# Sequence transform in one tile shape, alternating between the column halves

## The chip, the cores and the metric

One core of a Trainium2 chip. The metric is the time on the device, in microseconds, of one execution. Engines are called as the profile calls them: PE (TensorE matmul), PEld (its weight loads), DVE (VectorE), ACT (ScalarE), POOL (GpSimd), SP (the queue that issues transfers).

## The reference

Four batches, 1088 positions, 128 features (4 heads of 32). Three stages follow each other:

```python
# attention with a feature map, per head: phi(x) = (S1 x) outer (S2 x), 64 values
num = q_p @ (k_p.T @ v);  den = q_p @ sum(k_p);  x = num / (den + 1e-6)
# Fourier mixing and a channel block
X = np.fft.fft(np.fft.fft(x, axis=1), axis=2)      # over positions, then features
u = x + np.real(X)
x = u + relu(norm(u) @ w_ch1) @ w_ch2
# gated block with a spatial product over the 1088 positions
h = relu(x @ w_in);  a, v = h[..., :512], h[..., 512:]
out = (a * (w_spatial @ norm(v) + b_spatial)) @ w_out
```

All is float32. The scale factors of S1, S2 come as float64.

## The kernel before

The kernel first converts its weights from float64 bit patterns (`from_f64`, `weight`, on ACT, DVE and POOL), then runs for every batch `keys` and `queries` (the attention), `fourier_seq` and `fourier_feat` (the real part of the two-dimensional Fourier transform), `channel` and `spatial`. The attention and Fourier parts of batches 1 to 3 run early, and PE's gaps there are filled with products of the spatial part of batch 0 (tile `ac`, lines 569 to 571); the engines' instruction order is fixed when the program is built. Later batches interleave `channel(b + 1)` with `spatial(b)`, which runs to the end.

The Fourier part uses symmetry. Tokens s, S - s, 544 - s and 544 + s are kept together ("four groups"), so that sums and differences fold the position axis to a quarter, in an even and an odd parity, and the feature axis to 64 cosine and 63 sine columns and one extra column (feature 64). `fourier_seq` works like this (lines 404 to 453):

- line 408: a product folds the 9th row block (`rp`), ACT copies it to `rs_` (line 412);
- lines 417 to 434: DVE and POOL make the sums and differences: `eo`, `fe`, then `l_` (cosine part `l_[:, 0]`, sine part `l_[:, 1]`, by parity and row block), `lz` (the extra column, 32 wide), `lr` and `lzr` (leftover positions: 64 rows, of which each product takes 32). Line 415 and 416 zero a column of `l_` and of `lr` for each batch, on POOL;
- lines 438 to 453: for each parity nine products into `dps` (name `dft`), in 274 columns: for each of two row blocks a cosine product (128 rows, 64 columns, left half of the array), a sine product (right half) and the extra column (128 rows, 32 columns, at column 96); then the same three for the leftover positions, with 32 rows. ACT copies the result to every second column of `tb` (line 453).

`fourier_feat` (lines 455 to 475) multiplies `tb` by the feature table `dd` and adds the result to `ub`. In the profile each float32 matmul is two instructions, each with its weight load. `xtile` gives PSUM tiles: tag `acc` (two buffers) for batch 0, tag `x` (three) for the others. `warm` issues products of zeros that keep the clock up.

Positions are stored in the order of `_token_rows`; the host arranges inputs, tables (`_layout`) and the output by it.

Of the kernel before, what the change touches and what calls it, by code (L numbers as in the profile page):

```python
# [7 lines left out]
F32 = mybir.dt.float32  # L8
# [8 lines left out]
DM = 128  # L17
FF = 512
P = 128
NT = 9  # L20
CH = [(0, 384, 3), (384, 384, 3), (768, 320, 2)]
NCOL = 274
TW = 564
REM = [257 + i for i in range(15)] + [272, None, 0] + [None] * 14


def _groups(s):
    return [s % S, (S - s) % S, (544 - s) % S, (544 + s) % S]


def _token_rows():
    rows = []
    for blk in range(2):
        for g in range(4):
            rows += [_groups(1 + 128 * blk + i)[g] for i in range(128)]
    for g in range(4):
        rows += [_groups(257 if s is None else s)[g] for s in REM]
    return rows


def _rem_unique():
    return (
        [0 * 32 + i for i in list(range(16)) + [17]]
        + [1 * 32 + i for i in range(16)]
        + [2 * 32 + i for i in list(range(15)) + [17]]
        + [3 * 32 + i for i in range(15)]
    )

# [7 lines left out]
def fourier_attention_gmlp_kernel(  # L56
# [18 lines left out]
    nc = tc.nc  # L75
    V, A, T, G = nc.vector, nc.scalar, nc.tensor, nc.gpsimd
    mm = T.matmul
# [22 lines left out]
    ub, x2, marks = {}, {}, {}  # L100
# [4 lines left out]

    # spatial weights of one block of output positions, split into two float32r parts
    def spatial_load(pool, c, stage):
# [30 lines left out]

    # ------------------------------------------------------------------ channel part of one sequence
    def rstd(pool, mv, n, tag, nb=1):  # L140
# [134 lines left out]

    # ------------------------------------------------------------------ attention and Fourier mixing
    sa = ExitStack()
# [5 lines left out]
    trr = ca.tile([P, NCOL], F32, name="trr")  # L283
    dd = ca.tile([P, 2, DM], F32, name="dd")
    kvz = [ca.tile([P, 2, 66], F32, name=f"kvz{i}") for i in range(2)]
    lz = ca.tile([P, 2, 2, 32], F32, name="lz")
    lzr = ca.tile([64, 32], F32, name="lzr")
    tb = {}
# [6 lines left out]
    def from_f64(raw, n, out, fast):  # L295
        # mantissa rounded to float32 in [1, 2], times a power of two with the sign
        w = raw.rearrange("p (n two) -> p n two", two=2)
# [106 lines left out]
    def fourier_seq(b):  # L404
        # fold over the sequence, then over the features, then over the sequence halves
        xb = ub[b][:, 0:8, :].rearrange("p (k e f) d -> p (k e) f d", k=2, e=2)
        rp = xtile(b, [P, DM], "rp")
        mm(out=rp, lhsT=rfold, rhs=ub[b][:, 8, :], start=True, stop=True)
        if b == 0:
            warm(10)  # L410
        rs_ = ca.tile([P, DM], F32, tag="rs", name="rs_")
        A.copy(out=rs_, in_=rp)
        lr = ca.tile([P, 65], F32, tag="lr", name="lr")
        l_ = ca.tile([P, 2, 2, 2, 65], F32, tag="l_", name="l_")
        G.memset(l_[:, 1, :, :, 64:65], 0.0)
        G.memset(lr[64:128, 64:65], 0.0)
        for i, op in enumerate((ALU.add, ALU.subtract)):
            eo = ca.tile([P, 4, DM], F32, tag="eo", bufs=2, name="eo")
            V.tensor_tensor(out=eo, in0=xb[:, :, 0, :], in1=xb[:, :, 1, :], op=op)
            fe = ca.tile([P, 4, 64], F32, tag="fe", bufs=2, name="fe")  # L420
            if i == 0:
                G.tensor_copy(out=fe[:, :, 0:1], in_=eo[:, :, 0:1])
            V.tensor_tensor(out=fe[:, :, 1:64], in0=eo[:, :, 1:64], in1=eo[:, :, 127:64:-1], op=op)
            rows = slice(64 * i, 64 * i + 64)
            V.tensor_tensor(out=lr[rows, 1:64], in0=rs_[rows, 1:64], in1=rs_[rows, 127:64:-1], op=op)
            ev = fe.rearrange("p (k e) d -> p k e d", e=2)
            eov = eo.rearrange("p (k e) d -> p k e d", e=2)
            for par in range(2):
                o2 = ALU.add if par == i else ALU.subtract
                V.tensor_tensor(out=l_[:, i, par, :, i:64], in0=ev[:, :, 0, i:64], in1=ev[:, :, 1, i:64], op=o2)  # L430
                if i == 0:
                    G.tensor_tensor(out=lz[:, :, par, 31:32], in0=eov[:, :, 0, 64:65], in1=eov[:, :, 1, 64:65], op=o2)
        G.tensor_copy(out=lr[0:64, 0:1], in_=rs_[0:64, 0:1])
        G.tensor_copy(out=lzr[:, 31:32], in_=rs_[0:64, 64:65])
        t_ = tb[b] = ca.tile([P, TW], F32, tag="tb", bufs=2, name="tb")
        G.memset(t_[:, 548:TW], 0.0)
        tbv = t_[:, 0:550].rearrange("p (n two) -> p n two", two=2)
        for par in range(2):
            dps = xtile(b, [P, 512], "dft")
            for kt in range(3):  # L440
                for g in (0, 1, 2) if kt < 2 else (0, 2, 1):
                    cs = g % 2
                    q = slice(64 * cs + 32 * par, 64 * cs + 32 * par + 32)
                    if g < 2:
                        lh = l_[:, cs, par, kt, cs:64 + cs] if kt < 2 else lr[q, cs:64 + cs]
                    else:
                        lh = lz[:, kt, par, :] if kt < 2 else lzr[q, :]
                    rh = tr[:, kt, 2 * cs + par, :] if kt < 2 else trr[q, :]
                    o0, w = ((0, 64), (64, 64), (96, 32))[g]
                    mm(out=dps[o0:o0 + w, 0:NCOL], lhsT=lh, rhs=rh, start=(kt == 0 and g < 2),  # L450
                       stop=(kt == 2 and g < 2), tile_position=(0 if kt < 2 else q.start, o0))
            dst = tbv[:, 1:275, 0] if par == 0 else tbv[:, 0:274, 1]
            A.copy(out=dst, in_=dps[:, 0:NCOL])

    def fourier_feat(b):
        t_ = tb.pop(b)
        for blk in range(2):
            u_ = xtile(b, [P, 4, DM], "ups")
            for e in range(2):
                p0 = (275 if e else 1) + 128 * blk  # L460
                mm(
                    out=u_[:, 2 * e:2 * e + 2, :].rearrange("p g d -> p (g d)"),
                    lhsT=t_[:, p0:p0 + 128],
                    rhs=dd.rearrange("p g d -> p (g d)"),
                    start=True,
                    stop=True,
                )
            ux = ub[b][:, 4 * blk:4 * blk + 4, :]
            V.tensor_tensor(out=ux, in0=u_, in1=ux, op=ALU.add)
        u_ = xtile(b, [P, DM], "urm")  # L470
        for g in range(4):
            p0 = 257 if g < 2 else 531
            mm(out=u_[32 * g:32 * g + 32, :], lhsT=t_[:, p0:p0 + 32], rhs=dd[:, g % 2, :], start=True, stop=True,
               tile_position=(0, 32 * g))
        V.tensor_tensor(out=ub[b][:, 8, :], in0=u_, in1=ub[b][:, 8, :], op=ALU.add)
# [4 lines left out]
    A.activation(out=rt, in_=cst[:, 0:1], func=ACTF.Sqrt)  # L480
    # zero products that keep the tensor engine's clock up while it waits
    wz = a1
# [10 lines left out]
    from_f64(raw0, 64, sb_s, True)  # L493
    for z in (*kvz, lz, lzr):
        G.memset(z, 0.0)
# [52 lines left out]

    # ------------------------------------------------------------------ spatial part
    def spatial(b):  # L550
# [70 lines left out]
def _layout(q, k, v, S1, S2, moe_w_ch1, moe_w_ch2, moe2_w_in, moe2_w_spatial, moe2_b_spatial, moe2_w_out):  # L621
# [24 lines left out]
    a["wout"] = moe2_w_out.reshape(4, P, DM).transpose(1, 0, 2).reshape(P, FF)  # L646
    tpos = np.full(549, -1)
    for pos in range(1, 273):
        tpos[pos] = pos
    tpos[274] = 0  # L650
    for pos in range(275, 547):
        tpos[pos] = 818 - pos
    tpos[548] = 544
    lists = [tpos[2:549:2], tpos[1:549:2]]

# [11 lines left out]
    both = lambda ss: np.concatenate([table(ss, np.cos), table(ss, np.sin)], 1)  # L667
    full = both(list(range(1, 257))).reshape(2, P, 4, NCOL).transpose(1, 0, 2, 3)
    a["trig"] = full.astype(f32)
    a["trig_r"] = both(REM).transpose(1, 0, 2).reshape(P, NCOL).astype(f32)  # L670
    e = np.arange(P)
    dc = np.zeros((P, 2, P))
    for d in range(64):
        dc[d, :, :] = np.cos(2 * np.pi * ((d * e) % P) / P)
    for d in range(1, 64):
        sn = np.sin(2 * np.pi * ((d * e) % P) / P)
        dc[63 + d, 0, :] = -sn
        dc[63 + d, 1, :] = sn
    dc[127, :, :] = 1.0 - 2.0 * (e % 2)
    a["ddft"] = dc.astype(f32)  # L680
# [7 lines left out]
    for o in range(4):  # L688
        for g in range(4):
            for i in range(32):  # L690
                pm[32 * g + i, 2, 32 * o + i] = sgn[o, g]
    a["perm"] = pm
# [26 lines left out]
```

## Time and profile before

| | us |
|---|---|
| median of 3 runs | 484.94 |
| lowest and highest run | 482.51, 486.26 |
| span of the profiled execution (first to last instruction) | 481.6 |

The profiled execution's own time is given by its span alone; the runs are timed from outside. The profile is one execution, taken on the chip, with 7520 instructions. Busy times are sums over an engine's instructions, and matmuls overlap in the pipeline, so a busy PE is not PE at its peak. The chain of waits goes back from the last instruction to whatever released it. Times in the timeline count from the start of the span.

### The profile page before, as it was taken

To read this page: it belongs to the slowest core of one execution; us is meant where nothing else is said; L and a number is where in the kernel's file an instruction comes from. 1 tells how busy PE (TensorE), PEld (TensorE's weight loads), DVE (VectorE), ACT (ScalarE), POOL (GpSimd) and SP (SyncE) were. 2 spreads that over 40 slices of the span, in tenths; PEclk is the share of its full clock that TensorE was granted. 3 is DMA by queue.
4 is the path that set the end of the run, shared out by engine and by line. 5 is a ranking of instruction groups with operands and counts; after the bars stand their busy time and mean duration, and the time that the engine had idled before them with its cause. 6 is when DMAs were issued, how large, how long until landed. Compare 5 with 4: busy or idle time off the path is not lost.

```text
span 481.6 us, 7520 instructions
## 1 busy us (share of the span) xinstructions
PE 462.5 (96%) x2909; PEld 410.7 (85%) x2909; DVE 269.9 (56%) x677; ACT 193.0 (40%) x448; POOL 67.0 (14%) x105
## 2 busy tenths in 40 slices
PE   7889789999999997999999999999999999999996
PEld 6846678848948947989999999999999999999995
DVE  3576898849534518578963635496363547421221
ACT  3525687436322206445643333364243335311121
POOL 2044495426011104000000000000000000000000
PEclk9789899999999999899999999999999999999999
DMA  7950134004100004000000000000000000000000
GB/s 238 349 199 17 49 92 125 18 1 122 46 1 1 1 1 140 0 1 0 19 14 1 0 18 1 0 18 14 1 1 18 0 2 18 14 1 16 1 16 15
DMA packets 13007, 19.16 MB, mean 40 GB/s; under 512 B 1446, under 2 KB 11564, under 8 KB 12844
## 3 DMA queue, kind: packets, MB, share of 16 engines
q1 hardware_dynamic: 12972, 18.69, 12.2%
q8 instruction: 23, 0.38, 0.3%
q14 instruction: 12, 0.10, 0.1%
HBM read 16.45 MB, written 2.23 MB: 39 GB/s over the span
## 4 chain that ended last, share of the span: by engine, by line
PE 86%; DVE 5%; DMA 3%; ACT 2%; issue 1%; POOL 1%; SPq 1%; POOLq 0%; DVEq 0%; ACTq 0%
PE ac L569 13%; PE ac L571 13%; PE ac L570 13%; PE dft L450 8%; PE nm L387 3%; PE abp L331 2%; PE v_ps L244 2%; PE v_ps L246 2%; PE qps L376 2%; PE v_ps L245 2%; PE u_ps L564 2%; PE u_ps L562 2%; PE c L217 2%; PE ac L577 2%; PE ac L576 2%; PE u_ps L563 2%
## 5 line engine op out<-in xcount | busy, mean ns | idle before, releaser
L569 PE MATMUL ac<-wsh,vh 128*128 128x384 f32 (+1 forms) x384 | 126.9, 330 | 0.0
L571 PE MATMUL ac<-wsh,vlo 128*128 128x384 f32 (+1 forms) x384 | 126.6, 330 | 0.0
L570 PE MATMUL ac<-wsl,vh 128*128 128x384 f32 (+1 forms) x384 | 126.5, 330 | 0.0
L569 PEld LDWEIGHTS ac<-wsh,vh 128*128 128x128 f32 x384 | 72.2, 188 | 1.4 <-issue 0.8
L570 PEld LDWEIGHTS ac<-wsl,vh 128*128 128x128 f32 x384 | 72.2, 188 | 1.2 <-issue 0.4
L571 PEld LDWEIGHTS ac<-wsh,vlo 128*128 128x128 f32 x384 | 72.3, 188 | 1.2 <-issue 1.0
L580 DVE TENSOR_TENSOR uh<-ac,uh 128x384 f32<-128x384 f32 (+1 forms) x48 | 25.4, 530 | 55.5 <-PE ac L577 55.5
L566 ACT ACTIVATE uh<-u_ps 128x384 f32<-128x384 f32 (+1 forms) x48 | 22.6, 471 | 48.9 <-PE u_ps L564 46.9
L337 DVE TENSOR_TENSOR pp<-ab 128x768 f32<-128x768 f32 x23 | 26.1, 1150 | 17.5 <-ACT ab L333 16.5
L104 DVE TENSOR_TENSOR gl<-uh,gh 128x384 fp32r<-128x384 f32 (+1 forms) x48 | 25.6, 533 | 14.8 <-ACT gh L581 14.6
L235 POOL CAST xh<-xh 128x64 fp32r<-128x64 f32 x4 | 2.2, 543 | 202.2 <-ACT xh L232 202.2
L581 ACT CAST gh<-uh 128x384 fp32r<-128x384 f32 (+1 forms) x48 | 23.6, 492 | 10.8 <-DVE uh L580 10.5
L251 DVE BATCH_NORM_STATS2 bst<-vn 128x6 f32<-128x512 f32 x27 | 18.6, 693 | 16.7 <-ACT vn L249 16.6
L249 ACT ACTIVATE vn<-v_ps 128x512 f32<-128x512 f32 x27 | 16.0, 598 | 19.1 <-PE v_ps L246 18.6
L231 DVE TENSOR_TENSOR xt<-c,xt 128x384 f32<-128x384 f32 (+1 forms) x12 | 6.4, 530 | 27.4 <-PE c L217 27.4
L217 PE MATMUL c<-hl,w 128*128 128x384 f32 (+1 forms) x48 | 16.5, 345 | 1.1 <-DVE hl L210 1.1
L387 PE MATMUL nm<-kvz,qp 128*128 128x66 f32 x144 | 16.8, 274 | 0.0
L387 PEld LDWEIGHTS nm<-kvz,qp 128*128 128x128 f32 x144 | 16.7, 193 | 0.0
L272 ACT CAST vh<-vn 128x1024 fp32r<-128x1024 f32 x12 | 12.6, 1047 | 10.3 <-PE ac L570 8.3
L215 PE MATMUL c<-hh,w 128*128 128x384 f32 (+1 forms) x48 | 16.3, 340 | 0.0
L232 ACT CAST xh<-xt 128x384 fp32r<-128x384 f32 (+1 forms) x12 | 6.0, 497 | 25.7 <-DVE xt L231 25.7
L564 PE MATMUL u_ps<-sxl,wi 128*128 128x384 f32 (+1 forms) x48 | 15.9, 331 | 0.4 <-DVE sxl L104 0.4
(717 smaller groups left out, 961.1 us busy)
## 6 DMA issues: line engine op xcount, KB each, us to landing
wst<-in_wsp SPq DMA_DIRECT2D x18, 192.0 KB, 2.5
vx<-in_vt SPq DMA_DIRECT2D x12, 198.0 KB, 3.1
kt<-in_kT SPq DMA_DIRECT2D x12, 192.0 KB, 3.8
qt<-in_qT SPq DMA_DIRECT2D x12, 192.0 KB, 4.7
w2st<-in_wsp SPq DMA_DIRECT2D x9, 160.0 KB, 3.3
tr<-in_trig SPq DMA_DIRECT2D x1, 1096.0 KB, 8.4
wraw<-in_win SPq DMA_DIRECT2D x4, 256.0 KB, 6.3
wraw<-in_w SPq DMA_DIRECT2D x4, 256.0 KB, 4.9
```

The source lines that it names most:

```text
L104: eng.tensor_tensor(out=lo, in0=x, in1=hi.bitcast(F32), op=ALU.subtract)
L217: mm(out=c2[:, 0:n], lhsT=wpart("w2", 0, 128 * m, 128), rhs=hl[:, 0:n], start=False, stop=(m == 3))
L337: (G if [b, tag[0], c] in [[3, 'k', 2]] else V).tensor_tensor(out=pp, in0=a_.unsqueeze(3).to_broadcast([P, 12, 8, 8]), in1=b_.unsqueeze(2) ...
L387: mm(out=nm[:, t, 2 * pr:2 * pr + 2, :].rearrange("p h d -> p (h d)"), lhsT=qp[:, pr, 128 * t:128 * t + 128], rhs=z[:, pr, :], start=True, ...
L450: mm(out=dps[o0:o0 + w, 0:NCOL], lhsT=lh, rhs=rh, start=(kt == 0 and g < 2), stop=(kt == 2 and g < 2), tile_position=(0 if kt < 2 else q.s ...
L564: mm(out=h_[:, 0:n], lhsT=wpart("wi", 0, 128 * m, 128), rhs=xl[:, 0:n], start=False, stop=True)
L566: A.activation(out=uh[:, 0:n], in_=h_[:, 0:n], func=ACTF.Relu)
L569: mm(out=ac[:, 0:n], lhsT=vh[:, k, ms], rhs=wsh[c][:, k, :], start=(k == 0), stop=False)
L570: mm(out=ac[:, 0:n], lhsT=vh[:, k, ms], rhs=wsl[c][:, k, :], start=False, stop=False)
L571: mm(out=ac[:, 0:n], lhsT=vl[:, k, ms], rhs=wsh[c][:, k, :], start=False, stop=False)
L580: V.tensor_tensor(out=uh[:, 0:n], in0=ac[:, 0:n], in1=uh[:, 0:n], op=ALU.mult)
L581: A.copy(out=gh[:, 0:n], in_=uh[:, 0:n])
```

## The change

The position order is changed: the first 256 folded positions are split by parity (`MAIN`), the leftover ones are nine of each parity (`REST`), and the trigonometric tables, `perm` and `dd` are laid out anew on the host. Each parity then has a transform of its own with 274 columns stored one after the other in `tb[:, par, :]`.

The leftover operands are padded to 128 rows: `lrb` (zero outside the 32 rows of its part and parity) takes the place of `lr`, and `trr` is used whole. The extra column is moved into a 64 wide operand, in its last column (`lz`, 64 wide instead of 32; `lzr` goes). With the sine columns beginning at index 1 this makes every product 128 rows by 64 columns: three cosine products and five sine products for each parity, 16 in all instead of 18. They are issued in eight couples, one on the left half and one on the right half of the columns, in program order. Parity 1 has its sine part on the left and its cosine part on the right, so `dd` has a table for each parity. The copy of parity 0 stands after the fifth couple. The diff, cut to its core:

```diff
-    dd = ca.tile([P, 2, DM], F32, name="dd")
+    dd = ca.tile([P, 2, 2, DM], F32, name="dd")
-    lz = ca.tile([P, 2, 2, 32], F32, name="lz")
-    lzr = ca.tile([64, 32], F32, name="lzr")
+    lz = ca.tile([P, 2, 2, 64], F32, name="lz")
+    lrb = ca.tile([P, 2, 2, 64], F32, name="lrb")
...
-        lr = ca.tile([P, 65], F32, tag="lr", name="lr")
         l_ = ca.tile([P, 2, 2, 2, 65], F32, tag="l_", name="l_")
         G.memset(l_[:, 1, :, :, 64:65], 0.0)
-        G.memset(lr[64:128, 64:65], 0.0)
...
-            rows = slice(64 * i, 64 * i + 64)
-            V.tensor_tensor(out=lr[rows, 1:64], in0=rs_[rows, 1:64], in1=rs_[rows, 127:64:-1], op=op)
...
             for par in range(2):
...
+                rows = slice(64 * i + 32 * par, 64 * i + 32 * par + 32)
+                V.tensor_tensor(out=lrb[rows, i, par, 1 - i:64 - i], in0=rs_[rows, 1:64], in1=rs_[rows, 127:64:-1], op=op)
+                if i == 0:
+                    G.tensor_copy(out=lrb[rows, 0, par, 0:1], in_=rs_[rows, 0:1])
+                    G.tensor_copy(out=lrb[rows, 1, par, 63:64], in_=rs_[rows, 64:65])
-        G.tensor_copy(out=lr[0:64, 0:1], in_=rs_[0:64, 0:1])
-        G.tensor_copy(out=lzr[:, 31:32], in_=rs_[0:64, 64:65])
-        t_ = tb[b] = ca.tile([P, TW], F32, tag="tb", bufs=2, name="tb")
-        G.memset(t_[:, 548:TW], 0.0)
...
+        dps = [xtile(b, [P, 512], "dft") for _ in range(2)]
+        done = {}
+        def dft(par, sine, lhsT, rhs, last):
+            c0 = 64 * (sine ^ par)
+            m_ = mm(out=dps[par][c0:c0 + 64, 0:NCOL], lhsT=lhsT, rhs=rhs, start=(par, sine) not in done, stop=last,
+                    tile_position=(0, c0))
+            if done:
+                tc.keep_in_program_order(m_)
+            done[par, sine] = True
+        def cosines(par):
+            return [(par, 0, l_[:, 0, par, kt, 0:64], tr[:, kt, par, :], False) for kt in range(2)] + [
+                (par, 0, lrb[:, 0, par, :], trr, True)]
+        def sines(par):
+            return [(par, 1, l_[:, 1, par, kt, 1:65], tr[:, kt, 2 + par, :], False) for kt in range(2)] + [
+                (par, 1, lrb[:, 1, par, :], trr, False)] + [
+                (par, 1, lz[:, kt, par, :], tr[:, kt, par, :], kt == 1) for kt in range(2)]
+        tb[b] = ca.tile([P, 2, NCOL], F32, tag="tb", bufs=2, name="tb")
+        left, right = cosines(0) + sines(1), sines(0) + cosines(1)
+        for i, (x, y) in enumerate(zip(left, right)):
+            dft(*x)
+            dft(*y)
+            if i == 4:
+                A.copy(out=tb[b][:, 0, :], in_=dps[0][:, 0:NCOL])
+        A.copy(out=tb[b][:, 1, :], in_=dps[1][:, 0:NCOL])
...
-                    lhsT=t_[:, p0:p0 + 128],
-                    rhs=dd.rearrange("p g d -> p (g d)"),
+                    lhsT=t_[:, par, 146 * e:146 * e + 128],
+                    rhs=dd[:, par, :, :].rearrange("p g d -> p (g d)"),
...
-    nc = bacc.Bacc("TRN2", target_bir_lowering=False, num_devices=1)
+    nc = bacc.Bacc("TRN2", target_bir_lowering=False, num_devices=1, dynamic_dma_scratch_size=4096)
```

`lrb` is zeroed once at the start, as `lz` was.

## Rows read from the trace of the kernel before

**Rows 1.** The page, parts 1 and 4: busy engines, and the chain's shares.

```profile
PE 462.5 (96%) x2909; PEld 410.7 (85%) x2909; DVE 269.9 (56%) x677; ACT 193.0 (40%) x448; POOL 67.0 (14%) x105
PE 86%; DVE 5%; DMA 3%; ACT 2%; issue 1%; POOL 1%; SPq 1%; POOLq 0%; DVEq 0%; ACTq 0%
```

**Rows 2.** The chain of waits, start and length, first and last transform.

```profile
30.70 9.09 PE dft L450 x36
...
168.37 9.23 PE dft L450 x36
```

**Rows 3.** Windows, line 450 alone: length, PE, PEld, clock, DMA; last and sum.

```profile
168.30:177.60 9.30, 9.30 (x36) 2.80 (x36) 1.00 0.00 1
sum 39.10, PE 37.32 PEld 11.18; mean PE 9.33 PEld 2.79
```

**Rows 4.** Timeline of PE in batch 2: start, length, instructions, rows*columns, count.

```profile
136.56 0.68 PE L450 MATMUL dft<-tr,l__1452 128*64 128x274 f32 x4
137.18 0.65 PE L450 MATMUL dft<-tr,lz 128*32 128x274 f32 x2
137.75 0.67 PE L450 MATMUL dft<-trr,lr 32*64 32x274 f32 x2
138.35 0.64 PE L450 MATMUL dft<-trr,lzr 32*32 32x274 f32 x2
...
146.18 0.43 PE L473 MATMUL urm<-dd,tb 128*32 128x128 f32 x8
```

**Rows 5.** The same timeline in windows of 0.01 us, for single starts.

```profile
134.30 0.42 PE L450 MATMUL dft<-tr,l__1452 128*64 128x274 f32 x1
134.56 0.39 PE L450 MATMUL dft<-tr,l__1452 128*64 128x274 f32 x1
134.79 0.40 PE L450 MATMUL dft<-tr,l__1452 128*64 128x274 f32 x1
135.02 0.39 PE L450 MATMUL dft<-tr,l__1452 128*64 128x274 f32 x1
135.41 0.42 PE L450 MATMUL dft<-tr,l__1452 128*64 128x274 f32 x1
...
136.56 0.45 PE L450 MATMUL dft<-tr,l__1452 128*64 128x274 f32 x2
136.84 0.40 PE L450 MATMUL dft<-tr,l__1452 128*64 128x274 f32 x2
```

**Rows 6.** Timelines of batches 0 and 1: waits of POOL, DVE and ACT, in brackets.

```profile
39.90 0.09 POOL L416 MEMSET lr<- 64x1 f32 x1 [2.30 <-PE dft L450]
41.52 0.29 DVE L306 TENSOR_SCALAR ds<-wraw 128x256 int32<-128x256 int32 x1 [4.21 <-POOL dr L310]
...
106.93 0.41 ACT L453 COPY tb<-dft 128x274 f32<-128x274 f32 x1 [4.47 <-PE dft L450]
107.76 0.56 DVE L104 TENSOR_TENSOR wsl<-wst,wsh 128x384 fp32r<-128x384 f32 x1 [5.73 <-ACT wsh L124]
```

**Rows 7.** Weight loads, batch 2: timeline, and line 450's ns (least/median/most).

```profile
134.27 0.65 PEld L450 LDWEIGHTS dft<-tr,l__1452 128*64 128x64 f32 x4 [0.25 <-PE u_ps L563]
L450 PEld LDWEIGHTS dft<-tr,l__1452 x16: 132/136/138, 134.3 to 140.8; 128*64 128x64 f32 x16
```

**Rows 8.** Timelines: DVE ahead of the transform of batch 2; SP's issue of dd.

```profile
134.72 0.22 DVE L425 TENSOR_TENSOR lr<-rs__1449 64x63 f32<-64x63 f32 x1
134.97 0.49 DVE L430 TENSOR_TENSOR l__1452<-fe 128x126 f32<-128x126 f32 x2
15.21 0.35 SPq L513 DMA_DIRECT2D dd<-in_ddft  x1
```

**Rows 9.** Windows, all work: length, PE, PEld, DVE, ACT, POOL, clock, DMA, GB/s.

```profile
107.00:118.00 11.00, 10.52 (x107) 8.77 (x107) 10.00 (x12) 7.30 (x18) 8.57 (x9) 1.00 0.41 113
190.00:195.00 5.00, 2.56 (x14) 2.56 (x15) 3.13 (x9) 2.25 (x5) 1.22 (x2) 0.89 0.00 0
```

More of the change, by code (lines that the diff above doesn't have):

```diff
@@ L22, with _rest_tokens @@
 NCOL = 274
-TW = 564
-REM = [257 + i for i in range(15)] + [272, None, 0] + [None] * 14
+MAIN = [[2 + 2 * i for i in range(128)], [1 + 2 * i for i in range(128)]]
+REST = [[258 + 2 * i for i in range(7)] + [272, 0], [257 + 2 * i for i in range(8)] + [None]]
 def _groups(s):
     return [s % S, (S - s) % S, (544 - s) % S, (544 + s) % S]
+def _rest_tokens(par, v):
+    own = [_groups(257 if s is None else s) for s in REST[par]]
+    return [g[v] for g in own] + [g[2 + v] for g in own] + [257] * 14
 def _token_rows():
     rows = []
-    for blk in range(2):
+    for par in range(2):
         for g in range(4):
-            rows += [_groups(1 + 128 * blk + i)[g] for i in range(128)]
-    for g in range(4):
-        rows += [_groups(257 if s is None else s)[g] for s in REM]
+            rows += [_groups(s)[g] for s in MAIN[par]]
+    for par in range(2):
+        for v in range(2):
+            rows += _rest_tokens(par, v)
     return rows
 def _rem_unique():
[L42 to L47, printed above, removed]
+    seen, rows = set(), []
+    for par in range(2):
+        for v in range(2):
+            for i, t in enumerate(_rest_tokens(par, v)[:18]):
+                if REST[par][i % 9] is not None and t not in seen:
+                    seen.add(t)
+                    rows.append(64 * par + 32 * v + i)
+    return rows
 def _order():
@@ L431, in fourier_seq @@
                 if i == 0:
-                    G.tensor_tensor(out=lz[:, :, par, 31:32], in0=eov[:, :, 0, 64:65], in1=eov[:, :, 1, 64:65], op=o2)
-        G.tensor_copy(out=lr[0:64, 0:1], in_=rs_[0:64, 0:1])
-        G.tensor_copy(out=lzr[:, 31:32], in_=rs_[0:64, 64:65])
-        t_ = tb[b] = ca.tile([P, TW], F32, tag="tb", bufs=2, name="tb")
-        G.memset(t_[:, 548:TW], 0.0)
[L437 to L453, printed above, removed]
@@ new lines, in fourier_seq @@
+                    G.tensor_tensor(out=lz[:, :, par, 63:64], in0=eov[:, :, 0, 64:65], in1=eov[:, :, 1, 64:65], op=o2)
+                rows = slice(64 * i + 32 * par, 64 * i + 32 * par + 32)
[3 more added lines that the diff above has]
+                    G.tensor_copy(out=lrb[rows, 1, par, 63:64], in_=rs_[rows, 64:65])
@@ L455, in fourier_feat @@
+        A.copy(out=tb[b][:, 1, :], in_=dps[1][:, 0:NCOL])
     def fourier_feat(b):
         t_ = tb.pop(b)
-        for blk in range(2):
+        for par in range(2):
             u_ = xtile(b, [P, 4, DM], "ups")
             for e in range(2):
-                p0 = (275 if e else 1) + 128 * blk
                 mm(
                     out=u_[:, 2 * e:2 * e + 2, :].rearrange("p g d -> p (g d)"),
-                    lhsT=t_[:, p0:p0 + 128],
-                    rhs=dd.rearrange("p g d -> p (g d)"),
+                    lhsT=t_[:, par, 146 * e:146 * e + 128],
+                    rhs=dd[:, par, :, :].rearrange("p g d -> p (g d)"),
@@ L467, in fourier_feat @@
                 )
-            ux = ub[b][:, 4 * blk:4 * blk + 4, :]
+            ux = ub[b][:, 4 * par:4 * par + 4, :]
             V.tensor_tensor(out=ux, in0=u_, in1=ux, op=ALU.add)
         u_ = xtile(b, [P, DM], "urm")
[L471 to L474, printed above, removed]
+        for par in range(2):
+            for v in range(2):
+                o0 = 64 * par + 32 * v
+                mm(out=u_[o0:o0 + 32, :], lhsT=t_[:, par, 128:160], rhs=dd[:, par, v, :], start=True, stop=True,
+                   tile_position=(0, o0))
         V.tensor_tensor(out=ub[b][:, 8, :], in0=u_, in1=ub[b][:, 8, :], op=ALU.add)
@@ L493, in fourier_attention_gmlp_kernel @@
     from_f64(raw0, 64, sb_s, True)
-    for z in (*kvz, lz, lzr):
+    for z in (*kvz, lz, lrb):
         G.memset(z, 0.0)
@@ L646, in _layout @@
     a["wout"] = moe2_w_out.reshape(4, P, DM).transpose(1, 0, 2).reshape(P, FF)
[L647 to L654, printed above, removed]
+    lists = []
+    for par in range(2):
+        t = MAIN[par] + REST[par] + [None if s is None else 544 - s for s in REST[par]] + [544 - s for s in MAIN[par]]
+        lists.append(np.array([-1 if x is None else x for x in t]))
     def table(ss, fn):
@@ L667, in _layout @@
     both = lambda ss: np.concatenate([table(ss, np.cos), table(ss, np.sin)], 1)
-    full = both(list(range(1, 257))).reshape(2, P, 4, NCOL).transpose(1, 0, 2, 3)
+    full = both(MAIN[0] + MAIN[1]).reshape(2, P, 4, NCOL).transpose(1, 0, 2, 3)
     a["trig"] = full.astype(f32)
-    a["trig_r"] = both(REM).transpose(1, 0, 2).reshape(P, NCOL).astype(f32)
+    a["trig_r"] = both(REST[0] + REST[1] + [None] * 14).transpose(1, 0, 2).reshape(P, NCOL).astype(f32)
     e = np.arange(P)
[L672 to L679, printed above, removed]
+    cos = np.stack([np.cos(2 * np.pi * ((d * e) % P) / P) for d in range(64)])
+    sin = np.stack([np.sin(2 * np.pi * ((d * e) % P) / P) for d in range(1, 64)])
+    last = 1.0 - 2.0 * (e[None] % 2)
+    dc = np.zeros((P, 2, 2, P))
+    for v in range(2):
+        parts = [cos, (2 * v - 1) * sin, last]
+        dc[:, 0, v, :] = np.concatenate(parts)
+        dc[:, 1, v, :] = np.concatenate(parts[1:] + parts[:1])
     a["ddft"] = dc.astype(f32)
@@ L688, in _layout @@
     for o in range(4):
-        for g in range(4):
-            for i in range(32):
-                pm[32 * g + i, 2, 32 * o + i] = sgn[o, g]
+        for par in range(2):
+            for j in range(9):
+                for g in range(4):
+                    pm[64 * par + 32 * (g % 2) + 9 * (g // 2) + j, 2, 32 * o + 9 * par + j] = sgn[o, g]
     a["perm"] = pm
```

## The prediction

> **What bounds the kernel now.** I read the page first. PE is busy 462.5 of 481.6 us and carries 86% of the chain that ended last; no other engine is busy for more than 56% of the span [rows 1]. So time counts when it leaves PE, provided that PE doesn't then wait for a neighbour. The busy share alone doesn't prove this, because matmuls overlap and a matmul that takes twice too long looks just as busy. Next I followed the chain of waits in order of time: the sequence transform (line 450) stands on it in all four batches, almost without a break, from 30.70 to 39.79 us the first time and from 168.37 to 177.60 us the last [rows 2]. The windows over these four stretches give its price: 37.32 us of PE, 9.33 us a batch, at a granted clock of 1.00, the higher level of 2.4 GHz [rows 3]. The clock has nothing to give back there.
>
> Then I looked inside one transform, that of batch 2, in the timeline of PE [rows 4]. Each float32 matmul shows as two instructions, so 18 matmuls are 36. Two patterns are to be seen. A lone matmul between others of another shape (lz in 32 columns, lr over 32 rows, lzr over 32 rows by 32 columns) takes the engine 0.57 to 0.60 us before the next group can start: 137.18 to 137.75, 137.75 to 138.35. But where two matmuls of 128 rows by 64 columns follow each other, the cosine and the sine product of one row block, on different column halves, four instructions take 136.56 to 137.18, 0.62 us: no more than one. The starts show why [rows 5]: two instructions start together at 136.56 and the other two by 136.84. Where consecutive instructions work on the same half, they start 0.23 us apart (134.56, 134.79, 135.02). So 0.23 us is the work of one instruction, 0.46 that of one matmul, about 0.14 the price of a change of shape, and the two halves run side by side.
>
> The check on the sum: 36 instructions at 0.23 are 8.28; the two overlapping groups take off 2 x 0.46; some fourteen changes of shape at 0.14 add 1.96; that makes 9.32 against 9.33 measured. The transform's excess is thus changes of shape and halves that idle, not arithmetic.
>
> Last I looked at who stands behind it [rows 6]. In batch 1 ACT waits 4.47 us for the transform before it copies tb (line 453), the casts of the spatial weights are queued behind that copy, and DVE waits 5.73 us for those. In batch 0 POOL waits for dft twice (the memsets of l_ and lr for the next batch; the second wait is 2.30 us) and DVE then idles 4.21 us for POOL's weight conversion. These are queues held up by the transform, so a shorter one releases them too.
>
> **The change, part by part.** (a) The transform goes from 18 matmuls to 16 a batch: three for the cosines and five for the sines of each parity, all 128 rows by 64 columns, in eight couples, left half and right half in turn. With the halves side by side there are 16 instruction times of 0.23, 3.68 us; one half starts or ends alone, 0.23; one change of shape in and one out, at the 0.14 found above. That is 3.68 + 0.23 + 0.28 = 4.19 a batch, 16.8 in all (4 x 4.19), and 37.32 - 16.76 = 20.6 us saved. Bounds for one instruction time with both halves at work: 0.23 (a half can't go faster than alone) and 0.31 (0.62 / 2, the couple with its change of shape in it). The upper one gives back 16 x 0.08 x 4 = 5.1 us. I take 0.23, as most of the 0.62 is explained by the one change of shape. The eight instructions of line 473, over four column groups, bear it out: all eight lie within 0.43 us, where eight in a row of 128 columns would want 8 x 0.23 x 128 / 274 = 0.86 [rows 4].
>
> Against this stands a matter of weight loads. A load of 64 columns lasts 0.136 us, and the row of loads shows four of them from 134.27 to 134.92 while matmuls of the same rows start at 134.30, 134.56 and 134.79 [rows 5, 7]: they are hidden, and I cost them at nothing; without the cover they are 32 x 0.136 = 4.4 us a batch. The Trainium skill (TensorE: Matmul & The Clock Gate, Part 3, The mechanism) says that a weight load overlaps running matmuls only when its row group differs, and here all 32 instructions use all rows. By that rule each load would be paid in full and the time would be that of rival three below; the rows just named disagree with it.
>
> (b) The fixed order. The sine product now comes second, where before two cosine matmuls could go first. In batch 2 the first cosine starts at 134.30 and the sine operands were there at 135.41 [rows 5]. Now 0.46 us of work lies before that wait: 0.65 idle, against 0.16 already lost there before (135.41 - 135.02 - 0.23), so 0.5 more at most, and nothing where an ac matmul of the spatial part fills it. I take 0.4 a batch, 1.6 in all. Behind the waiting instruction stands all of PE.
>
> (c) Four lrb subtractions and additions of 32 rows take the place of two of 64, so two more a batch on DVE, one of them ahead of the sine operands. The price of one is between 0.1 (nothing but issue) and 0.25 (134.72 to 134.97, start of one to the next [rows 8]), the row lengths being equal. I take 0.25 for the one on the path, 1.0 in all; the other lies under the matmuls, and would cost as much without them.
>
> (d) POOL: memsets of lr and of tb go, two copies of one column come; eight small instructions before, eight after, so nothing in busy time. But the next batch's lr memset, which waited for the end of the transform, is gone, and the l_ memset is due after the fifth couple. That gain I leave in the bound (2.30 us of POOL a time [rows 6]).
>
> (e) The copy of parity 0 moves to after the fifth couple, and the two feature products of a block now need one parity alone. One copy is 0.41 us [rows 6]; PE fills that gap with other matmuls already, so nothing. The feature products, their adds and their count are as before.
>
> (f) dd doubles from 128 KB and the scratch argument becomes 4096. dd is issued at 15.21, far ahead of the transform's end at 39.7; SP issues it [rows 8], as the page's list of issues shows for every transfer; no row prices the scratch, and nothing here is issued from POOL. Nothing for either; the reads queued behind dd have no wait on the chain near it.
>
> Sum: 20.6 - 1.6 - 1.0 = 18.0 us. The page gives the profiled execution by its span alone, 481.6, so the span should become 463.6. The median of the runs is 484.94, 3.3 above that span, and I carry the 3.3 over: 484.94 - 18.0 = 466.9 us.
>
> **The rivals.** One: the gain is partly given back in batches 0 and 1, because DVE becomes the bound. For it: DVE is busy 10.00 of 11.00 us right after the transform of batch 1 [rows 9]. Against it: that is work held up until then, as the waits show, and it starts earlier too. If nothing of batch 0 (4.5) and half of batch 1 (2.3) comes through, the time is 466.9 + 6.8 = 473.7.
>
> Two: the halves don't run side by side when every matmul alternates and the target bank changes midway. Then 32 x 0.23 + 0.28 = 7.64 a batch, 6.8 saved in all, 2.6 lost to (b) and (c): 480.7. Against it stand the four instructions in 0.62 us.
>
> Three, on the other side: each weight load waits for the matmul running in the other half. Then 32 x (0.136 + 0.23) + 0.28 = 11.99 a batch, 48.0 against 37.3; with the 2.6 it ends at 484.94 + 13.3 = 498.2. It decides from a couple above 1.1 us on (9.33 / 8, less the losses), instead of 0.46. Against it are the overlapping loads of rows 7.
>
> Four, also slower: a change of half costs what a change of shape costs. Then 16 x 0.60 = 9.6 a batch, 38.4; 1.1 more and 2.6 lost: 488.6. Against it: within the couple at 136.56 the half changes and no such price appears.
>
> **How the numbers follow.** The forecast, 0.70; rival one, 0.13; two, 0.06; three, 0.04; four, 0.03; and 0.04 for more than forecast: none of the losses of (b) and (c) (2.6), POOL's 2.30 in a batch or two, and less of the PE gap before the channel part of batch 1, where PE is busy only 2.56 of 5.00 us after 190 us [rows 9]; 466.9 - 2.6 - 2.3 - 2.0 gives 460.0 as the low end. The high end: the upper bound in (a) (5.1) and half of batch 0 lost (2.2) make 474.2, rival one 473.7, and with some of (b) unfilled twice I take 476. The range 460 to 476 leaves out rivals two to four and the surplus, 0.17. One per cent (4.8 us, about the spread of the three runs) is what a measurement of this kernel can tell from no change. Faster by over 1%, that is below 480.1: forecast, surplus, rival one and a third of rival two, 0.89. Within 1%: the rest of two, 0.04. Slower: three and four, 0.07.
>
> **What the profile after would show.** The transform's chain pieces fall from 9.1 to 9.4 us to 4 to 4.5, with 32 instructions, all 128*64, and pairs starting together or 0.23 us in turn: (a) right. A piece near 7.6 means rival two, near 9.6 or 12 rivals four or three. An idle row of PE released by DVE l_ inside the transform is the price of (b). ACT's 4.47 and DVE's 4.21 and 5.73 us of idle time shrink if the queues behind are released; if the pieces shrink but the stage from 40 to 118 us doesn't end 9 us earlier, it was rival one. I am wrong on the sum, though right on the mechanism, if instructions are re-sorted so that PE waits for DVE elsewhere.

## The result

The changed kernel takes 468.1 us (median of 4 runs, 467.33 to 468.66) where the kernel before takes 483.73 in the same comparison (481.69 to 486.26): a ratio of 0.966, 95% interval 0.961 to 0.970. A second comparison gave 467.96 and again 0.966 (0.962 to 0.970). 466.9 had been forecast, so the time lies in the range, and the gain is 15.6 us where 18.0 was forecast.

The page of the changed kernel, parts 1 and 4:

```profile
span 465.7 us, 7498 instructions
PE 444.4 (95%) x2893; PEld 410.0 (88%) x2893; DVE 276.3 (59%) x685; ACT 192.3 (41%) x448; POOL 65.5 (14%) x105
PE 71%; issue 9%; DVE 7%; ACT 5%; POOL 3%; DMA 3%; SPq 1%; POOLq 0%; DVEq 0%; ACTq 0%
```

The windows over its transforms alone (line 451; columns as in [rows 3]; first, last and sum):

```profile
28.60:35.10 6.50, 4.45 (x32) 2.77 (x32) 1.00 0.33 122
...
157.40:162.80 5.40, 4.55 (x32) 2.38 (x32) 1.00 0.02 5
sum 28.90, PE 18.08 PEld 10.28; mean PE 4.52 PEld 2.57
```

PE spends 18.08 us in the transforms instead of 37.32 [rows 3]; its share of the chain falls from 86% to 71% [rows 1], and DVE, ACT and POOL take more of it. The timeline of PE within batch 2's transform, instruction by instruction:

```profile
130.92 0.39 PE L451 MATMUL dft<-tr,l__1449 128*64 128x274 f32 x1
131.12 0.39 PE L451 MATMUL dft<-trr,lrb 128*64 128x274 f32 x1
131.16 0.39 PE L451 MATMUL dft<-tr,l__1449 128*64 128x274 f32 x1
131.35 0.39 PE L451 MATMUL dft<-tr,lz 128*64 128x274 f32 x1
131.39 0.39 PE L451 MATMUL dft<-tr,l__1449 128*64 128x274 f32 x1
131.58 0.39 PE L451 MATMUL dft<-tr,lz 128*64 128x274 f32 x1
```

Two chains are interleaved, each with a start every 0.23 us: the two halves, each at the pace that one half alone had in [rows 5]. Nothing waits for weight loads.

Where the gain arises is seen by comparing the moments at which PE begins and leaves each transform (starts from the timelines of both kernels, us; "ahead" is before minus after):

| | before | after | ahead |
|---|---|---|---|
| product rp of batch 0 | 26.35 | 25.65 | 0.7 |
| transform 0 ends (next instruction) | 39.70 | 35.10 | 4.6 |
| transform 1 begins | 95.67 | 92.44 | 3.2 |
| transform 1 ends | 106.82 | 100.19 | 6.6 |
| transform 2 begins | 134.30 | 128.51 | 5.8 |
| transform 2 ends | 143.68 | 133.75 | 9.9 |
| transform 3 begins | 168.30 | 157.42 | 10.9 |
| transform 3 ends | 177.53 | 162.60 | 14.9 |
| span ends | 481.6 | 465.7 | 15.9 |

Each of transforms 1 to 3 brings 3.4 to 4.1 us. 1.4 us are lost between transforms 0 and 1, and 0.8 between 1 and 2; 1.0 is gained between 2 and 3, and another 1.0 behind transform 3. The 0.7 at rp of batch 0 can't be put down to the change: a second profile of the changed kernel has this product at 26.23. What takes the place of the old waits is seen in the waits of PE (total, times, longest):

```profile
PE dft L451 <- DVE l__362 L436: 2.0, 1, 2.0
PE ups L480 <- ACT tb L473: 1.9, 2, 1.0
```

and in the timeline of POOL, DVE and PE just ahead of transform 2, first before, then after the change:

```profile
133.29 0.39 POOL L434 COPY lzr<-rs__1449 64x1 f32<-64x1 f32 x1
133.63 0.20 POOL L422 COPY fe<-eo 128x4 f32<-128x4 f32 x1
...
133.86 0.49 DVE L430 TENSOR_TENSOR l__1452<-fe 128x128 f32<-128x128 f32 x2
```

```profile
126.71 0.39 POOL L442 COPY lrb<-rs__1447 32x1 f32<-32x1 f32 x1 [20.34 <-ACT rs__1447 L422]
127.04 0.39 POOL L443 COPY lrb<-rs__1447 32x1 f32<-32x1 f32 x1
127.49 0.18 POOL L442 COPY lrb<-rs__1447 32x1 f32<-32x1 f32 x1
127.61 0.18 POOL L443 COPY lrb<-rs__1447 32x1 f32<-32x1 f32 x1
127.84 0.19 POOL L430 COPY fe<-eo 128x4 f32<-128x4 f32 x1
128.07 0.49 DVE L436 TENSOR_TENSOR l__1449<-fe 128x128 f32<-128x128 f32 x2 [0.56 <-POOL fe L430]
...
128.51 0.65 PE L451 MATMUL dft<-tr,l__1449 128*64 128x274 f32 x2 [0.42 <-DVE l__1449 L436]
```

POOL's four copies for the leftover operand, 126.71 to 127.84, stand ahead of the one copy (into fe, line 430) that DVE's first l_ needs; DVE and then PE wait for it. Before the change only two copies stood there (at 132.96 and 133.29), and DVE's row shows no wait for fe.

### The profile page after: what moved, and what is told of

The parts are those of the page before. It is cut to its first block, busy times and chain, and to the rows that moved or that the text cites. A ratio compares the mean times of both kernels' runs of the same rounds, so it can differ in the third digit from the quotient of the medians.

```text
span 465.7 us, 7498 instructions
## 1 busy us (share of the span) xinstructions
PE 444.4 (95%) x2893; PEld 410.0 (88%) x2893; DVE 276.3 (59%) x685; ACT 192.3 (41%) x448; POOL 65.5 (14%) x105
## 3 DMA queue, kind: packets, MB, share of 16 engines
HBM read 16.58 MB, written 2.23 MB: 40 GB/s over the span
## 4 chain that ended last, share of the span: by engine, by line
PE 71%; issue 9%; DVE 7%; ACT 5%; POOL 3%; DMA 3%; SPq 1%; POOLq 0%; DVEq 0%; ACTq 0%
PE ac L590 12%; PE ac L591 12%; PE ac L589 12%; PE v_ps L256 2%; PE dft L451 2%; PE v_ps L254 2%; PE c L227 2%; PE v_ps L255 2%; PE ac L597 1%; PE ac L596 1%; PE u_ps L582 1%; PE c L225 1%; PE u_ps L583 1%; PE u_ps L584 1%; PE c L226 1%
## 5 line engine op out<-in xcount | busy, mean ns | idle before, releaser
L259 ACT ACTIVATE vn<-v_ps 128x512 f32<-128x512 f32 x27 | 16.0, 598 | 19.2 <-PE v_ps L256 18.7
L256 PE MATMUL v_ps<-wi,xl 128*128 128x512 f32 x36 | 15.3, 425 | 1.1 <-DVE xl L114 1.1
L582 PE MATMUL u_ps<-sxh,wi 128*128 128x384 f32 (+1 forms) x48 | 16.2, 338 | 0.0
```

Source lines behind the costliest of these rows:

```text
L256: mm(out=h_, lhsT=xl[:, cs], rhs=wt["wi"][:, 2:4, 0, :], start=False, stop=True)
```

## The experiments

All were timed against runs of the kernel before on the same chip. The theory: (a) the halves run side by side; changes of shape cost; and the leftover operands and the early sine product give a part back. The rivals: the new shape alone, the scratch argument, or the released queues.

**One half after the other.**

```diff
-        for i, (x, y) in enumerate(zip(left, right)):
-            dft(*x)
+        for x in left:
+            dft(*x)
+        for i, y in enumerate(right):
             dft(*y)
```

> All eight products of the left half come first, then all eight of the right half: the shapes stay equal, the halves no longer overlap. Theory (the halves run side by side): a transform becomes 32 x 0.23 + 0.3 = 7.7 us instead of the 4.5 of the changed kernel, so about 3.1 us more in each of four batches, 480.5 us in all. Rival (the gain comes from equal shapes alone): no difference, 468 us.

Measured: 475.24 us, ratio 0.980 (0.974 to 0.987), against 0.966. PE in transforms: 27.56 us, 6.89 a batch instead of 4.52. So the shape alone is not the gain, and the halves' overlap is worth 9.5 us of PE (27.56 - 18.08). The expected 7.7 a batch was too high because the engine overlaps by itself what stands close. The timeline of PE in batch 2, where the left half's last products (lz) and the right half's first (l_) meet:

```profile
133.74 0.39 PE L451 MATMUL dft<-tr,lz 128*64 128x274 f32 x1
133.75 0.45 PE L451 MATMUL dft<-tr,l__1449 128*64 128x274 f32 x1
133.97 0.39 PE L451 MATMUL dft<-tr,lz 128*64 128x274 f32 x1
134.03 0.39 PE L451 MATMUL dft<-tr,l__1449 128*64 128x274 f32 x1
```

The right half's first four instructions, written behind all of the left's, ran beside the left's last four. Also PE waits nowhere for the sine operands in batch 0, as the cosines of parity 0 come first. Both speak for a smaller loss than the 12 us expected; it was 7.1.

**The extra column narrow again.**

```diff
-            c0 = 64 * (sine ^ par)
+            c0, w = 64 * (sine ^ par), lhsT.shape[-1]
+            c0 += 64 - w
...
-                (par, 1, lrb[:, 1, par, :], trr, False)] + [
-                (par, 1, lz[:, kt, par, :], tr[:, kt, par, :], kt == 1) for kt in range(2)]
+                (par, 1, lz[:, kt, par, 32:64], tr[:, kt, par, :], False) for kt in range(2)] + [
+                (par, 1, lrb[:, 1, par, :], trr, True)]
```

> The changed kernel, with the extra column as a product of 32 columns again (four of the sixteen products of a batch), ahead of the leftover product. Theory (each change of shape drains the engine, and a product between two changes stands alone): four couples of 0.46 us become two lone products of 0.60 each, 4 x (1.20 - 0.46) = 3.0 us a batch, 480 us in all. Rival (only the halves matter, and the new shape costs nothing by itself): 468 us. Both this and the run with one half after the other slower would mean that the two effects are not additive but one needs the other.

Measured: 476.52 us, ratio 0.983 (0.977 to 0.989). The timeline of PE in batch 2:

```profile
136.63 0.65 PE L452 MATMUL dft<-tr,lz 128*32 128x274 f32 x2
137.21 0.68 PE L452 MATMUL dft<-tr,l__1449 128*64 128x274 f32 x2
137.81 0.65 PE L452 MATMUL dft<-tr,lz 128*32 128x274 f32 x2
138.39 0.45 PE L452 MATMUL dft<-tr,l__1449 128*64 128x274 f32 x1
138.40 0.45 PE L452 MATMUL dft<-trr,lrb 128*64 128x274 f32 x1
```

Four products of sixteen in the other shape cost 8.4 us: a lone one again takes 0.58 to 0.60 us, and the half beside it idles (137.21 to 137.81). Undisturbed batches take 7.00 us of PE, 2.5 more than the changed kernel's 4.52; 3.0 had been expected, and some products paired up anew (138.39 and 138.40). So shape and alternation both count: the alternation undone, or four of sixteen products in the other shape, gives back about half of the gain. The two losses add up to 15.5 us (7.1 + 8.4), about the whole gain, so it isn't shown that the one effect needs the other, as the expectation would have it.

**The scratch argument alone**, added to the kernel before.

> The kernel before with the scratch argument of the changed one and nothing else. Theory: no transfer uses it, so the time is that of the kernel before, within 0.5%. Rival: part of the gain is the argument's, 482 us or less.

Measured: 485.14 us, ratio 0.999 (0.996 to 1.003). By itself it has no effect that these runs can tell.

**The kernel before, grouped by shape.** Nothing is padded; a list gives the order, and both copies stand at the end.

```diff
+        plan = [(par, kt, g) for par in range(2) for kt in range(2) for g in range(2)]
+        plan += [(par, kt, 2) for par in range(2) for kt in range(2)]
+        plan += [(par, 2, 2) for par in range(2)]
+        plan += [(par, 2, g) for par in range(2) for g in range(2)]
+        for n, (par, kt, g) in enumerate(plan):
```

> The kernel before with its eighteen products of a batch grouped by shape: eight of 128 rows by 64 columns in couples over the halves, then the four of 32 columns, the two of 32 by 32, the four of 32 rows; nothing padded, both copies at the end. Theory (order, not arithmetic, carries the price): 4 x 0.46 + 4 x 0.46 + 2 x 0.46 + 2 x 0.46 + 4 x 0.14 = 6.1 us a batch and less if row groups overlap, against 9.3, so 12 to 14 us off, about 472 us, most of the gain without padding. Rival: the padding is needed, 480 us or more.

Measured: 471.55 us, ratio 0.977 (0.972 to 0.982): two thirds of the gain by the ratios (0.023 of 0.034), and 12.3 of 15.6 us by the medians, without a zero row added. The transforms take 23.72 us of PE, 5.93 a batch. The timeline of PE in batch 2:

```profile
131.90 2.03 PE L452 MATMUL dft<-tr,lz 128*32 128x274 f32 x8
133.86 0.65 PE L452 MATMUL dft<-trr,lzr 32*32 32x274 f32 x4
134.44 0.69 PE L452 MATMUL dft<-trr,lr 32*64 32x274 f32 x8
```

The narrow products, all on the same columns, run in turn: 1.96 us for eight instructions. The four leftover products of 32 rows, on four places of the array, take 0.63 together.

**Two buffers for l_ and lr in the kernel before**, to free POOL of its wait.

```diff
-        lr = ca.tile([P, 65], F32, tag="lr", name="lr")
-        l_ = ca.tile([P, 2, 2, 2, 65], F32, tag="l_", name="l_")
+        lr = ca.tile([P, 65], F32, tag="lr", bufs=2, name="lr")
+        l_ = ca.tile([P, 2, 2, 2, 65], F32, tag="l_", bufs=2, name="l_")
```

> The kernel before with two buffers for l_ and lr (and the scratch argument, for their room): POOL's memsets for the next batch no longer wait for the transform, all else is as before. Theory: the freed queue gives back DVE's idle 4.2 us of batch 0 only in part, as ACT's copy still waits for the transform: 1 to 3 us less than before, 483 us. Rival: the released POOL queue was a main part of the change's gain: 478 us or less. Second rival: nothing, since DVE's work there has slack.

Measured: 484.15 us, ratio 1.002 (0.999 to 1.005). It settles nothing, since the wait stayed. POOL and DVE in batch 0:

```profile
35.53 0.11 POOL L415 MEMSET l__1452<- 128x4 f32 x1 [3.35 <-PE dft L450]
37.95 0.09 POOL L416 MEMSET lr<- 64x1 f32 x1 [2.30 <-PE dft L450]
...
39.56 0.29 DVE L306 TENSOR_SCALAR ds<-wraw 128x256 int32<-128x256 int32 x1 [4.20 <-POOL dr L310]
```

With a second buffer the memset of a batch later was put into the same place and waits just as long. What the released queue is worth stays open.

**No leftover operands.** The eight instructions that fill lrb are left out, so the leftover positions are missing from the transform; the products still run, on zeros.

```diff
-                V.tensor_tensor(out=lrb[rows, i, par, 1 - i:64 - i], in0=rs_[rows, 1:64], in1=rs_[rows, 127:64:-1], op=op)
-                if i == 0:
-                    G.tensor_copy(out=lrb[rows, 0, par, 0:1], in_=rs_[rows, 0:1])
-                    G.tensor_copy(out=lrb[rows, 1, par, 63:64], in_=rs_[rows, 64:65])
```

> The changed kernel without the eight small instructions a batch that fill lrb (four on DVE, four on POOL), so the leftover positions are left out of the transform; all products still run. Theory (c): one DVE instruction a batch lies on the path at 0.25 us, so about 1 us less than the changed kernel, 467 us. Rival: POOL's four copies stand ahead of the products in its queue and set the start of the transform in batches 1 to 3, then 2 to 4 us less, 465 us.

Measured: 461.28 us, ratio 0.955 (0.952 to 0.958). About 5 to 7 us hang on these eight small instructions (0.966 - 0.955 of 484, or the difference of the medians), where the prediction had 1.0. The rival is nearer. In batch 2 the copy into fe now comes at once, and the transform runs without a wait:

```profile
123.84 0.52 POOL L430 COPY fe<-eo 128x4 f32<-128x4 f32 x1 [18.23 <-DVE eo L427]
...
124.89 0.89 DVE L436 TENSOR_TENSOR l__1433<-fe 128x128 f32<-128x128 f32 x4
125.46 1.14 PE L446 MATMUL dft<-tr,l__1433 128*64 128x274 f32 x7
```

All four l_ are made in one stretch from 124.89, where the changed kernel has 128.07 to 128.56 for the first two and 129.50 to 129.99 for the others. It leaves open whether the place or the time of the instructions costs. Five more versions, each with all the work, bear on that.

**Two cosine couples first.**

```diff
-        left, right = cosines(0) + sines(1), sines(0) + cosines(1)
+        left, right = cosines(0) + sines(1), cosines(1)[0:2] + sines(0) + cosines(1)[2:3]
...
-            if i == 4:
+            if i == 6:
```

> The changed kernel with two cosine couples (parity 0 left, parity 1 right) ahead of the first sine product, and the copy of parity 0 after the seventh couple. Theory (b, the wait for the sine operands costs about 0.4 us a batch, and 2.0 in the trace of batch 0): 1 to 2 us less, 466.5 us. Rival: DVE's chain, not PE's order, sets when the sine products can run, and the later copy costs as much again: 468 us or more.

Measured: 464.97 us, ratio 0.960 (0.955 to 0.965). The largest wait for sine operands, 2.0 us in batch 0, is gone; the first eight instructions run before one is needed. Of the 3.2 us between the two profiles' spans (465.7 and 462.5), 1.2 lie ahead of rp of batch 0 and can't be the order's; the table at the end of this section leaves them out.

**The same, with the sums for lrb on POOL.**

```diff
-                V.tensor_tensor(out=lrb[rows
+                G.tensor_tensor(out=lrb[rows
```

> The version with two cosine couples first, and the four lrb sums and differences on POOL in place of DVE. Theory (DVE is the bound of batches 0 and 1): 0.5 to 1 us less than that version, 464 us. Rival: POOL is slower at them and ends later than the products need them, 466 us or more.

Measured: 465.62 us, ratio 0.964 (0.961 to 0.967): no gain, so moving the sums to POOL is not the remedy; the time lies just under the rival's 466. POOL, DVE and PE ahead of transform 3, with seven of the eight lrb instructions between 156.22 and 158.34, ahead of fe:

```profile
158.03 0.31 POOL L440 TENSOR_TENSOR lrb<-rs__1683 32x63 f32<-32x63 f32 x1
158.41 0.19 POOL L430 COPY fe<-eo 128x4 f32<-128x4 f32 x1
...
158.63 1.02 DVE L436 TENSOR_TENSOR l__1685<-fe 128x128 f32<-128x128 f32 x4 [1.31 <-POOL fe L430]
...
159.07 1.31 PE L451 MATMUL dft<-tr,l__1685 128*64 128x274 f32 x8 [1.11 <-DVE l__1685 L436]
```

A longer queue ahead of fe makes DVE wait 1.31 us and PE 1.11. So this run doesn't tell what DVE's time alone is worth, as POOL's queue grew with it.

**The fill of lrb written behind l_ and lz**, products as in the changed kernel: the four lines above move to a loop of their own ahead of `dps`.

> The changed kernel with the eight small instructions that fill lrb written behind those of l_ and lz; the products and their order are as in the changed kernel. Theory (the price of the leftover operands is their place in the queues, since POOL's four copies and DVE's sums stand ahead of l_, and without them the kernel was 5 to 7 us faster): 2 to 4 us less, 465 us. Rival (their price is DVE's and POOL's time, wherever they stand): no difference, 468 us.

Measured: 465.75 us, ratio 0.962 (0.958 to 0.966), beside the changed kernel itself, run once more as their measure.

> The changed kernel once more, on the same chip as the two below, as their measure: a ratio to the kernel before of 0.966, as found at first.

Measured for that: 467.96 us, ratio 0.966 (0.962 to 0.970). So the later fill brings 2.2 us with the same instructions on the same chip, as the theory had it. In batch 2:

```profile
127.27 0.19 POOL L430 COPY fe<-eo 128x4 f32<-128x4 f32 x1
...
127.49 0.89 DVE L436 TENSOR_TENSOR l__1449<-fe 128x128 f32<-128x128 f32 x4 [0.44 <-POOL fe L430]
...
128.31 0.93 DVE L444 TENSOR_TENSOR lrb<-rs__1447 32x63 f32<-32x63 f32 x4
```

DVE's sums now stand behind l_, but POOL still takes its four copies (126.03 to 127.21) ahead of fe: the place in the text doesn't settle the place in the queue, which is chosen when the program is built.

**Also the leftover couples last**: two cosine couples, then sines and extra column, then the leftover products.

> The same, with two cosine couples first, then the sines and the extra column, and the two leftover couples last, the copy of parity 0 after the seventh couple. Theory: both waits are covered (sine operands by 0.9 us of work, leftover operands by 2.8 us), so the time falls below that of two cosine couples alone (465.0) and near that without leftover work (461.3): 462 us, the fastest with all the work done. Rival: DVE is the bound of batches 0 and 1, 465 us.

Measured: 464.49 us, ratio 0.959 (0.955 to 0.964). That is 1.3 us below the version before, and nearer to the rival's 465 than to 462. In batches 2 and 3 the first product still comes 2.65 us behind rp, as there or slightly later.

**And POOL's copies held behind fe and lz.**

```diff
-                G.tensor_copy(out=fe[:, :, 0:1], in_=eo[:, :, 0:1])
+                first = G.tensor_copy(out=fe[:, :, 0:1], in_=eo[:, :, 0:1])
...
+                    with tc.issue_after(first.ins):
+                        G.tensor_copy(out=lrb[rows, 0, par, 0:1], in_=rs_[rows, 0:1])
+                        G.tensor_copy(out=lrb[rows, 1, par, 63:64], in_=rs_[rows, 64:65])
```

> The version with the leftover couples last, and POOL's four lrb copies held behind its copy into fe and the lz sums: before that, POOL still took the four copies first, and DVE's l_ waited for fe. Theory (it is the place in POOL's queue that costs): a start of the transform about 0.8 us earlier in each batch, 462 us, near the 461.3 without the leftover instructions. Rival (DVE's four sums a batch are what remains): no difference to the version it is made from, 464.5 us.

Measured: 460.41 us, ratio 0.949 (0.946 to 0.952): the fastest, with all the work done, 1.7% below the changed kernel. Ahead of the transform of batch 2:

```profile
123.16 0.52 POOL L430 COPY fe<-eo 128x4 f32<-128x4 f32 x1 [20.24 <-DVE eo L427]
...
124.20 0.89 DVE L436 TENSOR_TENSOR l__1449<-fe 128x128 f32<-128x128 f32 x4
124.76 2.11 PE L454 MATMUL dft<-tr,l__1449 128*64 128x274 f32 x16
```

and its transforms, by windows (length, PE, clock, DMA):

```profile
115.00:145.00 30.00, 3.96 (x32) 1.00 0.03 8
sum 145.00, PE 16.05; mean PE 4.01
```

The copies' time is still spent; only their place changed. From rp to the first product of transform 2 it takes 2.23 us, against 2.65 in the version before, 2.55 in the changed kernel and 2.09 before the change.

But not all of the 4 us between the last two medians is the copies' place. Their profiled spans differ by 3.0 us (461.1 and 458.1), and 1.4 of it is there at rp of batch 0 already, although the instructions ahead of it are the same in the same order on PE, DVE, ACT and POOL. What differs most is the granted clock from 10 to 24 us, 0.76 with the leftover couples last and 0.88 with the copies held (columns as in [rows 9], in this order):

```profile
10.00:24.00 14.00, 12.59 (x122) 12.09 (x119) 6.79 (x18) 6.82 (x18) 0.75 (x2) 0.76 1.04 382
10.00:24.00 14.00, 10.68 (x100) 10.05 (x96) 6.88 (x22) 7.26 (x19) 1.46 (x2) 0.88 1.03 374
```

Eighteen products there (`abp`) take 4.04 us in the one and 2.59 in the other. Why the clock differs there isn't shown. So it is safer to count from rp of batch 0 to the end of transform 3 (starts from the timelines, us):

| | rp of batch 0 | transform 3 ends | between |
|---|---|---|---|
| kernel before | 26.35 | 177.53 | 151.18 |
| changed kernel | 25.65 | 162.60 | 136.95 |
| changed kernel, second profile | 26.23 | 163.07 | 136.84 |
| two cosine couples first | 24.44 | 159.26 | 134.82 |
| lrb filled behind l_ and lz | 25.89 | 160.06 | 134.17 |
| also the leftover couples last | 25.99 | 159.34 | 133.35 |
| and POOL's copies held | 24.63 | 156.21 | 131.58 |
| no leftover operands | 26.48 | 157.84 | 131.36 |

Two profiles of one kernel agree within 0.1 us in this count. Taken one after the other, the place of DVE's sums brings 2.7 us, the order of the products another 0.8 (2.1 by itself, without the leftover couples last), and the place of POOL's copies 1.8: 5.3 us together, at no change in work, and the version without the leftover operands is hardly faster. So it was the place, in the queues and in the order of the products. Of the last 1.8 us, 0.7 are earlier starts of transforms 2 and 3; some 0.7 lie between transforms 0 and 1, and their cause wasn't found.

## Why the prediction was right, and where it was off

**The mechanism of (a) held, and its size nearly.** 32 instructions at 0.23 us for two, 4.52 us of PE a batch against 4.19; the 0.33 more is mainly the first cosine product, which now runs alone and is cut off from the rest by ac products (128.51, then 129.94), so that one more half idles and the shape changes twice more. In the version with everything in order, 4.01 a batch is below the forecast. Rivals two, three and four fell: the halves overlap (kept apart they need 27.56 us instead of 18.08); weight loads stay hidden as in [rows 7], although all products use all rows; and a change of half costs nothing, while a change of shape does.

**(b) did not come as forecast.** In batches 2 and 3 ac products fill the wait for the sine operands; the 0.4 us seen there is PE's wait for the first cosine operand, a matter of (d). In batch 0 PE waited 2.0 us for the sine operands, where 0.4 had been taken. But that is no loss of 2.0, as the same place in the two profiles of the changed kernel shows, the first one first:

```profile
31.30 0.88 PE L451 MATMUL dft<-tr,l__362 128*64 128x274 f32 x5 [2.00 <-DVE l__362 L436]
```

```profile
31.87 0.88 PE L451 MATMUL dft<-tr,l__362 128*64 128x274 f32 x5 [0.72 <-DVE l__362 L436]
```

In the second, PE comes later: ten products ahead of the transform (`wp`) take 3.77 us at a granted clock of 0.74 (25 to 30 us), and 2.55 at 1.00 in the first. Yet the transform ends 9.45 us behind rp in both. DVE sets that end: it has the last sine operand ready 5.7 us behind rp in both, against 5.1 before the change.

**(c) and (d) are the step that failed.** "Eight before, eight after, so nothing" counts busy time, and what matters is where they stand in their queues. The prediction took one DVE instruction of 0.25 us a batch for all of it, 1.0 in all, and nothing for POOL; removing them brought 5 to 7 us, and putting them behind what the first product needs, with the products in a fitting order, brought as much (5.3 us counted from rp, 7.5 by the medians). From rp to the last sine operand DVE takes 5.7, 6.5, 4.0 and 4.0 us in the four batches, against 5.1, 5.9, 3.3 and 3.6 before: 2.3 us more, where 1.0 had been forecast. The row that should have been read is the one of POOL before, shown with the result: its copy into fe is what releases l_, behind two copies then, behind four now.

**(e) was wrong by a little.** The copies into tb were costed at nothing, but ACT now has other work in its queue ahead of the second copy, and PE waits 1.9 us for it in batches 0 and 1 (0.99 and 0.91).

**(f) held**: 0.999 for the scratch argument alone; dd is waited for nowhere.

**The queues behind the transform** were released as expected where they could be seen. In batch 0 POOL's memset of l_ (36.38) no longer waits for the transform, and DVE's idle 4.21 us [rows 6] is gone. In batch 1 DVE begins the wsl split at 99.19 instead of 107.76, and DVE's wait for ACT's casts falls from 5.73 us [rows 6] to 0.7 in two. This is why rival one came true only in part, with 1.4 us lost between transforms 0 and 1 and 0.8 between 1 and 2, instead of 6.8. By the prediction's own sign the stage to 118 us should have ended 9 us earlier; transform 2 begins 5.8 earlier. How much POOL's freed queue adds isn't shown, as the run with two buffers left the wait in place.

So the total came out near because the main term, 19.2 us of PE against 20.6 forecast, was sized within 1.4 us, and the rest, 2.6 us forecast, was 3.6 in the end (19.2 - 15.6). The gain is off by 2.4 us, the time by only 1.2; that was luck, as the forecast counted from 484.94 and the kernel before took 483.73 in the comparison.

## What to carry to other kernels

Small matmuls of one tile shape on different column halves ran side by side here, and each change of shape cost 0.12 to 0.14 us and left the other half idle; so group by shape first (here two thirds of the gain) and pad only what remains. When the bound engine gets faster, look at once at the queue order of the small instructions that make its first operands: here their place and the order of the products were worth 5 us and more beside a gain of 15.6, at no change in work. A second buffer freed no queue here, as the builder moved the next wait into the same place.

## What the runs showed of the hardware

PE started instructions for an idle half ahead of older ones for a busy half: four instructions written after the left half's last ones ran beside them. Products of 32 rows on different rows and halves overlapped as well: eight instructions in 0.63 us, against 0.23 for one. And the narrow shape cost more in batch 0 (8.45 us of PE against 7.00), where PE had idled 2.01 us for l_. The windows of that kernel (the extra column narrow), columns as in [rows 9]:

```profile
29.90:32.50 2.60, 0.65 (x2) 0.17 (x2) 2.48 (x7) 0.44 (x1) 0.70 (x1) 0.97 0.22 82
32.50:35.70 3.20, 3.13 (x11) 1.09 (x11) 3.20 (x12) 1.93 (x4) 0.84 (x1) 0.50 0.00 0
```

The seventh column is the granted clock: 0.50, behind the idle stretch, is the lower level, 1.2 GHz. The changed kernel idled as long at the same place (2.00 us) and kept 1.00 behind it, so such an idle stretch is followed by the lower clock in one profile and not in another. The two profiles of the changed kernel, one and the same program, differ as well: 1.00 and 0.74 from 25 to 30 us.
